# Starting a gated linear attention: the first unit's gates by chunks, with the second unit's steps in their gaps

## The chip, the cores and the metric

The kernel runs on one core of one Trainium2 chip, in float32. The metric is the device time of one execution in microseconds (us). The median of three runs of the kernel before is 581.96 us (580.95 to 583.16).

## The reference, cut to what matters

Two blocks are chained. The first is a gated recurrence over 768 steps for 4 batches of 8 heads of 48 channels, with a complex gate for each channel. The second is a mixture of eight experts, of which each token takes one.

```python
def _attn_ref(q, k, v, a_re, a_im):
    mag = np.sqrt(a_re * a_re + a_im * a_im)
    scale = np.minimum(mag, 0.999) / (mag + 1e-06)
    a_re_n, a_im_n = (a_re * scale, a_im * scale)
    for t in range(S):
        ar, ai = (a_re_n[:, :, t, :, None], a_im_n[:, :, t, :, None])
        new_re = ar * S_re - ai * S_im
        new_im = ar * S_im + ai * S_re
        kv = np.einsum('bhd,bhe->bhde', k[:, :, t], v[:, :, t])
        S_re, S_im = (new_re + kv, new_im)
        y[:, :, t] = np.einsum('bhd,bhde->bhe', q[:, :, t], S_re)

def _moe_ref(x, w_gate, w1, w2):
    logits = x @ w_gate
    expert_idx = np.argmax(logits, axis=1)
    ...                                    # softmax weight of the chosen expert
    for e in range(E):                     # the tokens sorted by expert
        h = np.maximum(x_sorted[lo:hi] @ w1[e], 0.0)
        y_sorted[lo:hi] = h @ w2[e]
    return gate_w[:, None] * y
```

## The kernel before

The recurrence is computed in blocks of 128 steps. A chunk is one block of one batch: 128 steps by 8 heads by 48 channels, which is 384 columns. A unit is two chunks (two batches), W = 768 columns, and there are 12 units. For every unit the kernel needs the running sums of the gate's logarithm and of its angle within the block; both come from a product of TensorE with a triangular matrix. From them follow a decay E with its inverse Ei, and a cosine and sine CS; with these q and k become Q and K, and scores and outputs are matmuls.

The steps of a unit's gates are these. A becomes the logarithm of the capped magnitude, ai the tangent of the angle and later the angle.

```python
    def decay_steps(u):
        ar, ai = T["ar", u], T["ai", u]
        A = un.tile([P, W], FP, tag="A", name="A")
        R = un.tile([P, W], FP, tag="R", name="R", bufs=1)
        T["L", u], T["th", u] = A, ai
        def s0():
            act(out=A, in_=ar, func=AF.Ln)
        def s1():
            act(out=R, in_=A, func=AF.Exp, scale=-1.0)
            nc.vector.tensor_tensor(out=ai, in0=ai, in1=R, op=OP.mult)
            act(out=R, in_=ai, func=AF.Square)
        def s2():
            act(out=R, in_=R, func=AF.Ln, bias=1.0)
            nc.vector.scalar_tensor_tensor(out=A, in0=A, scalar=2.0, in1=R, op0=OP.mult, op1=OP.add)
        def s3():
            act(out=R, in_=A, func=AF.Exp, scale=-0.5, bias=ln2e6)
            nc.vector.scalar_tensor_tensor(out=A, in0=A, scalar=LN_CAP2, in1=R, op0=OP.min, op1=OP.subtract)
        return [s0, s1, s2, s3]

    def decay_angle(u):
        act(out=th, in_=th, func=AF.Arctan)
        ...
    def decay_sums(u, c):                  # chunk c; psM has one buffer
        cs = psM.tile([P, DM], FP, tag="mm", padded_shape=[P, 512], name="csl")
        mm(cs, tri_half, T["L", u][:, sl])
        act(out=T["E", u][:, sl], in_=cs, func=AF.Exp)
        act(out=T["Ei", u][:, sl], in_=cs, func=AF.Exp, scale=-1.0)
        ...
    def angle_sums(u, c):
        cs = psM.tile([P, DM], FP, tag="mm", padded_shape=[P, 512], name="cst")
        mm(cs, tri_turn, T["th", u][:, sl])
        ...                                # r = rounded cs, f = cs - r (DVE)
        if c == U - 1:
            ...                            # fa = |f| over the whole unit (DVE)
    def rotation(u):
        act(out=CS[:, :, 0], in_=fa, func=AF.Sin, scale=2.0 * math.pi, bias=mhalfpi)
        act(out=CS[:, :, 1], in_=f, func=AF.Sin, scale=2.0 * math.pi)
```

ScalarE has one table of functions for logarithm and exponential and another for arctangent and sine. `table(...)` switches it, and the helper `act` keeps the activations of gates in program order. One pass of the loop handles the sums of unit u, the gates of unit u + 1, and the scores of unit u - 1:

```python
    load_a(0)
    load_qkv(0)
    ...                                    # w_gate
    load_a(1)
    table("natural_log_exp_and_others")
    for f in decay_steps(0):
        f()
    table("trig_and_small")
    decay_angle(0)
    for u in range(NU + 1):
        if 0 < u < NU:
            load_qkv(u)
        ...
        if u < NU:
            steps = decay_steps(u + 1) if u + 1 < NU else []
            steps = steps[:1] + [lambda: decay_sums(u, 0)] + steps[1:2] + [lambda: decay_sums(u, 1)] + steps[2:]
            table("natural_log_exp_and_others")
            for i, f in enumerate(steps):
                f()
                ...
            for c in range(U):
                angle_sums(u, c)
            table("trig_and_small")
            rotation(u)
            if u + 1 < NU:
                decay_angle(u + 1)
        ...
        for c in range(U):
            g = (u - 1) * U + c
            if g >= 0:
                scores(g)                  # transposes of Q and K (copies qt, kt), at, am, dk
            if u < NU:
                decayed(u, c)              # Qe = q * E, Ke = k * Ei (DVE)
            if g > 0:
                outputs(g - 1)
        ...
        if u + 2 < NU:
            load_a(u + 2)
```

In `scores` VectorE first multiplies Qe and Ke with CS, which gives Q and K. After the twelve units the tokens' rows, sorted by expert through memory, are loaded again (xg), and the eight experts run as matmuls named hps and yps.

Of the kernel before, what the change touches and what calls it, by code (L numbers as in the profile page):

```python
# [10 lines left out]
FP = mybir.dt.float32  # L11
I32 = mybir.dt.int32
BF = mybir.dt.bfloat16
AF = mybir.ActivationFunctionType
OP = mybir.AluOpType
# [5 lines left out]
P = 128  # L21
MAGIC = 12582912.0
LN_CAP2 = 2.0 * math.log(0.999)
# [14 lines left out]
def kernel(  # L38
# [12 lines left out]
    nc = tc.nc  # L51
    B, H, S, D = q.shape
    DD = 2 * D
    DM = H * D
# [3 lines left out]
    NT = N // P  # L58
    CB = S // P
    U = 2  # L60
    NU = NT // U
    W = U * DM
# [27 lines left out]
    def const(shape, name, dt=FP):  # L90
        return cp.tile(shape, dt, name=name)
# [15 lines left out]
    mhalfpi = const([P, 1], "mhalfpi")  # L107
    nc.vector.memset(mhalfpi, -0.5 * math.pi)

    ln2e6 = const([P, 1], "ln2e6")  # L110
# [47 lines left out]
    T, W_T = {"put": []}, {}  # L158
# [56 lines left out]
    ld = att.enter_context(tc.tile_pool(name="ld", bufs=2))  # L215
    un = att.enter_context(tc.tile_pool(name="un", bufs=2))
# [8 lines left out]
    def act(**kw):  # L225

        ins = nc.scalar.activation(**kw)
        if "act" in T:
            queue(ins, T["act"])
        T["act"] = ins  # L230
# [10 lines left out]
            queue(ins, T["act"])  # L241
        T["act"] = ins

    def load(u, names):
        for nm, src in names:
            if nm == "v":
                t = vbuf[u % 3][:, :, :, 0:D]
                T[nm, u] = vbuf[u % 3]
            else:
                t = ld.tile([P, U, H, D], FP, tag=nm, name=nm, bufs=3 if nm == "ai" else 2)  # L250
                T[nm, u] = t.rearrange("p c h d -> p (c h d)")
            s, b = divmod(u * U, B)
            T["ld"] = nc.sync.dma_start(
                out=t.rearrange("p c h d -> p (c h) d"),
                in_=src[b : b + U, :, s * P : (s + 1) * P, :].rearrange("b h t d -> t (b h) d"),
            )

    def load_a(u):
        load(u, (("ar", a_re), ("ai", a_im)))

    def load_qkv(u):
        load(u, (("q", q), ("k", k), ("v", v)))

    def decay_steps(u):

        ar, ai = T["ar", u], T["ai", u]
        A = un.tile([P, W], FP, tag="A", name="A")
        R = un.tile([P, W], FP, tag="R", name="R", bufs=1)
        T["L", u], T["th", u] = A, ai

        def s0():
# [14 lines that stand above are left out]
            nc.vector.scalar_tensor_tensor(out=A, in0=A, scalar=LN_CAP2, in1=R, op0=OP.min, op1=OP.subtract)  # L286

        return [s0, s1, s2, s3]

    def decay_angle(u):  # L290

        th = T["th", u]
        act(out=th, in_=th, func=AF.Arctan)
        if u * U >= B:
            T["c0", u] = un.tile([96, 8], FP, tag="c0", name="c0")
            nc.gpsimd.dma_start(out=T["c0", u], in_=th[0:1].rearrange("o (p j) -> o p j", j=8))
# [10 lines left out]
    def decay_sums(u, c):  # L307
        sl = slice(c * DM, (c + 1) * DM)
        if c == 0:
            T["E", u] = un.tile([P, W], FP, tag="E", name="E", bufs=1)  # L310
            T["Ei", u] = un.tile([P, W], FP, tag="Ei", name="Ei", bufs=1)
        cs = psM.tile([P, DM], FP, tag="mm", padded_shape=[P, 512], name="csl")
        mm(cs, tri_half, T["L", u][:, sl])
        act(out=T["E", u][:, sl], in_=cs, func=AF.Exp)
        act(out=T["Ei", u][:, sl], in_=cs, func=AF.Exp, scale=-1.0)
        s, b = divmod(u * U, B)
        if s < CB - 1 and c == U - 1:
            if b == 0:
                T["er", s] = un.tile([B, H, 2, D], FP, tag="er", name="er")
            for a in range(2):  # L320
                nc.gpsimd.dma_start(
                    out=T["er", s][b : b + U, :, a],
                    in_=T["E", u][P - 1 : P].rearrange("p (c h d) -> p c h d", c=U, d=D),
                )
# [8 lines left out]
        T["M", s] = un.tile([P, B, H], FP, tag="M", name="M")  # L333
        nc.scalar.copy(out=T["M", s][0:DD], in_=mt[0:DD].rearrange("p h b -> p b h"))

    def angle_sums(u, c):

        if c == 0:
            for nm in ("f", "fa"):
                T[nm, u] = un.tile([P, W], FP, tag=nm, name=nm, bufs=1)  # L340
        sl = slice(c * DM, (c + 1) * DM)
        f = T["f", u][:, sl]
        cs = psM.tile([P, DM], FP, tag="mm", padded_shape=[P, 512], name="cst")
        mm(cs, tri_turn, T["th", u][:, sl])
        r = ch.tile([P, DM], FP, tag="r", name="r")
        nc.vector.tensor_scalar(out=r, in0=cs, scalar1=MAGIC, scalar2=MAGIC, op0=OP.add, op1=OP.subtract)
        nc.vector.tensor_tensor(out=f, in0=cs, in1=r, op=OP.subtract)
        if c == U - 1:
            f, fa = T["f", u], T["fa", u]
            nc.vector.tensor_scalar(  # L350
                out=fa.bitcast(I32), in0=f.bitcast(I32), scalar1=0x7FFFFFFF, scalar2=None, op0=OP.bitwise_and
            )
            if (u + 1) * U <= NT - B:
                T["fl", u] = un.tile([96, 8], FP, tag="fl", name="fl", bufs=3)
                nc.gpsimd.dma_start(out=T["fl", u], in_=f[P - 1 : P].rearrange("o (p j) -> o p j", j=8))

    def rotation(u):

# [6 lines left out]
    def decayed(u, c):  # L365

        sl = slice(c * DM, (c + 1) * DM)
        for nm, src, dec in (("Q", "q", "E"), ("K", "k", "Ei")):
            e = T[nm, u, c] = ch.tile([P, H, D], FP, tag=nm + "e", name=nm + "e")
            o = e.rearrange("p h d -> p (h d)")  # L370
            nc.vector.tensor_tensor(out=o, in0=T[src, u][:, sl], in1=T[dec, u][:, sl], op=OP.mult)
# [170 lines left out]
            nc.sync.dma_start(out=xg[0 : sizes[f], f], in_=rows[:, f * P :].rearrange("o p c -> (o p) c"))  # L542
        return xg

    load_a(0)
    load_qkv(0)
    for z in range(2):
        nc.sync.dma_start(
            out=wg[z * DP : z * DP + D, :, 0:E],
            in_=w_gate.rearrange("(i z d) e -> z d i e", z=2, d=D)[z],  # L550
        )
    load_a(1)
    table("natural_log_exp_and_others")
    for f in decay_steps(0):
        f()
    table("trig_and_small")
    decay_angle(0)
    def place():

        if T["put"]:  # L560
            T["put"].pop(0)()

    for u in range(NU + 1):
        if 0 < u < NU:
            load_qkv(u)
        for i in range(NS // (P * BL)):
            if 2 + i * 2 // (NS // (P * BL)) == u:
                blank(i)
# [7 lines that stand above are left out]
                if i == 1:  # L576
                    carry_angle(u)
            for f in T.pop("chosen", []):
# [7 lines that stand above are left out]
        else:  # L586
            table("natural_log_exp_and_others")
            choose(NT - 2 * GR, GR)()
            T["put"] += route(NT - 2 * GR, False)
            while T["put"]:  # L590
                place()
        if u < NU:
            place()
        for f in T.pop("route", []):
            T["put"] += f()
        for c in range(U):
            g = (u - 1) * U + c
            if g >= 0:
                scores(g)
            if u < NU:  # L600
                decayed(u, c)
            if g > 0:
                outputs(g - 1)
        for _ in range(2 if u >= NU - 2 else 1):
            place()
        if u > 2 and u % 2 and u < NU - 1:

            j = (u - 3) * U
            T["chosen"] = [choose(j, GR)]
            T["route"] = [lambda j=j: route(j, False)]  # L610
        if u + 2 < NU:
            load_a(u + 2)
        if u == NU - 1:
            experts_at(range(2), True)
            load_w(0, range(KD + KF // 2))
# [327 lines left out]
```

## Time and profile before

The engines are PE (TensorE matmul), PEld (its weight loads), DVE (VectorE), ACT (ScalarE), POOL (GpSimd) and SP (SyncE, which issues the loads). Times are us from the start of the profiled execution, whose span is 581.7 us.

| part | what the trace shows |
|---|---|
| until 30 us | gates of units 0 and 1, first loads; no scores yet |
| 30.15 us | first transpose of scores on PE |
| 30 to about 285 us | attention units, one after another |
| 284.55 us | first load of rows for the experts (xg) |
| 288 to 582 us | experts |

A line of the timeline gives the start, the duration, the engine, the line of the program, the operation with its output and input tiles and their shapes, how often it stands there, and in brackets how long the engine was idle before it and what ended the idle time. ACT_TABLE_LOAD is the switch of ScalarE's table; the execution has 27 of them. A row of digits cuts the span into 40 slices of 14.5 us and gives the busy share of each in tenths.

### The profile page before, as it was taken

Reading aid. Unit: us, or ns where it says so; the run is one execution under the profiler, and the core shown is the slowest. Engines: PE = TensorE matmul, PEld = TensorE weight load, DVE = VectorE, ACT = ScalarE, POOL = GpSimd, SP = SyncE. Lnnn points to the kernel's source line nnn. Section 1 sums busy time; section 2 is a strip of 40 time slices with the busy share of each in tenths; the row PEclk is TensorE's granted clock in tenths of the full one; section 3 lists DMA queues with packets and bytes.
Section 4 is the critical chain, followed back from the end, with each engine's and each line's share of the span. In section 5 each row is a group of like instructions: output and inputs, shape, how many; then the busy total and the mean of one; then the engine's idle time right before and its main releaser. Section 6 shows DMA issues by size and latency. Waiting matters only on the chain.

```text
span 581.7 us, 8539 instructions
## 1 busy us (share of the span) xinstructions
PE 538.5 (93%) x3264; PEld 366.0 (63%) x3264; DVE 263.8 (45%) x604; ACT 281.6 (48%) x476; POOL 129.8 (22%) x148
## 2 busy tenths in 40 slices
PE   1499999989999999999799999999999999999995
PEld 0177677678778788687577655555555555555553
DVE  2568877687888879876231211211213022020210
ACT  5677977767777777744210116125162351715210
POOL 2101211231231230201121004215043150604201
PEclk9999999989999999999889999999999999999999
DMA  9999993926854732610443563642736426380001
GB/s 159 182 233 236 257 129 48 177 75 107 150 112 72 135 83 54 231 45 27 152 162 100 177 219 122 210 146 79 271 122 223 153 67 250 122 283 15 25 2 41
DMA packets 151586, 79.31 MB, mean 136 GB/s; under 512 B 127830, under 2 KB 143087, under 8 KB 151536
## 3 DMA queue, kind: packets, MB, share of 16 engines
q1 hardware_dynamic: 146672, 69.04, 50.3%
q0 software_dynamic: 4864, 9.63, 4.9%
q8 instruction: 28, 0.46, 0.4%
q14 instruction: 22, 0.18, 0.1%
HBM read 63.30 MB, written 15.54 MB: 136 GB/s over the span
## 4 chain that ended last, share of the span: by engine, by line
PE 46%; DMA 2%; issue 1%; POOL 1%; ACT 1%; DVE 1%; POOLq 0%; DVEq 0%
PE hps L79 23%; PE yps L79 20%; PE tp L643 2%; DMA xs<-x,slot 2%; POOL cai L732 1%; POOL cs L729 1%; DMA xg<-xs 1%; DVE xt L82 0%; ACT cw L725 0%; ACT cs L725 0%; ACT cai L725 0%; ACT xt L82 0%; DVE y L689 0%; POOL out_dram L654 0%; POOLq L909 0%
## 5 line engine op out<-in xcount | busy, mean ns | idle before, releaser
L79 PE MATMUL hps<-xt,w1t 128*128 128x416 f32 (+4 forms) x432 | 137.5, 478 | 0.0
L79 PE MATMUL yps<-w2t,ht 128*128 128x384 f32 (+2 forms) x464 | 135.1, 487 | 0.0
L79 PEld LDWEIGHTS hps<-xt,w1t 128*128 128x128 f32 x432 | 81.1, 193 | 50.6 <-issue 30.2
L79 PEld LDWEIGHTS yps<-w2t,ht 128*128 128x128 f32 (+2 forms) x464 | 76.3, 178 | 56.7 <-issue 7.4
L674 ACT ACTIVATE ht<-hps 128x416 f32<-128x416 f32 (+4 forms) x36 | 17.1, 475 | 126.9 <-PE hps L79 126.9
L689 DVE TENSOR_SCALAR y<-yps,xg 128x384 f32<-128x384 f32 x24 | 14.8, 617 | 117.3 <-PE yps L79 117.3
L678 DVE TENSOR_SCALAR ht<-hps 128x416 f32<-128x416 f32 (+4 forms) x36 | 19.4, 539 | 90.9 <-PE hps L79 90.7
L79 PE MATMUL at<-qt,kt 96*128 96x128 f32 x384 | 54.9, 285 | 3.5 <-DVE kt L82 2.8
L79 PEld LDWEIGHTS at<-qt,kt 96*128 96x128 f32 x384 | 49.2, 195 | 9.9 <-DVE kt L82 3.3
L79 PE MATMUL y<-am,v 128*64 128x128 f32 x384 | 51.6, 289 | 0.4 <-DVE am L484 0.3
L454 POOL DMA_INDIRECT xs<-x,slot x24 | 26.2, 1094 | 106.7 <-DMA xs<-x,slot 38.3
L654 POOL DMA_INDIRECT out_dram<-y,xg x29 | 28.0, 966 | 92.7 <-DVE y L689 43.7
L79 PE MATMUL y<-qt,G 96*64 96x128 f32 x320 | 46.5, 284 | 0.0
L729 POOL TENSOR_TENSOR cs<-cs,cw 128x768 f32<-128x768 f32 x12 | 21.6, 1804 | 95.8 <-ACT cw L725 95.8
L484 DVE TENSOR_TENSOR am<-at,tri 128x512 f32<-128x512 f32 x48 | 33.0, 686 | 16.9 <-PE at L79 16.6
L79 PE MATMUL csl<-A,tri_half 128*128 128x384 f32 x48 | 24.3, 591 | 17.2 <-DVE A L286 12.8
L79 PEld LDWEIGHTS y<-am,v 128*64 128x64 f32 x384 | 33.8, 138 | 9.5 <-issue 7.8
L79 PEld LDWEIGHTS y<-qt,G 96*64 96x64 f32 x320 | 33.5, 139 | 3.5 <-issue 2.7
L476 PE MATMUL tp<-ident,Q 128*96 128x128 f32 x192 | 33.7, 285 | 2.0 <-DVE Q L376 2.0
L239 ACT ACT_TABLE_LOAD x27 | 34.6, 1283 | 1.2 <-PEq L929 0.8
L82 ACT COPY qt<-tp 96x512 f32<-96x512 f32 x48 | 27.8, 580 | 15.1 <-PE tp L476 14.8
L79 PEld LDWEIGHTS dk<-v,K 128*96 128x96 f32 x320 | 31.0, 170 | 3.8 <-DVE t L514 1.5
(144 smaller groups left out, 747.0 us busy)
## 6 DMA issues: line engine op xcount, KB each, us to landing
w1t<-in_moe_w_dram SPq DMA_DIRECT2D x7, 1536.0 KB, 6.4
w2t<-in_moe_w_dram SPq DMA_DIRECT2D x7, 1536.0 KB, 7.2
xs<-zrow SPq DMA_DIRECT2D x7, 772.0 KB, 8.8
ar<-in_a_re_dram SPq DMA_DIRECT2D x12, 384.0 KB, 5.8
ai<-in_a_im_dram SPq DMA_DIRECT2D x12, 384.0 KB, 6.4
q<-in_q_dram SPq DMA_DIRECT2D x12, 384.0 KB, 6.1
k<-in_k_dram SPq DMA_DIRECT2D x12, 384.0 KB, 6.4
v<-in_v_dram SPq DMA_DIRECT2D x12, 384.0 KB, 4.4
```

Of the source, the lines that this page charges most:

```text
L79: return nc.tensor.matmul(o, lhsT=lhsT, rhs=rhs, start=start, stop=stop, skip_group_check=True)
L82: (nc.scalar.copy if i % 2 else nc.vector.tensor_copy)(out=o, in_=in_)
L239: ins = nc.scalar.preload_act_table_set(name)
L454: pool(nc.gpsimd.indirect_dma_start(out=xs[:, :], out_offset=bass.IndirectOffsetOnAxis(ap=to[:, i : i + 1], axis=0), in_=x[:, i], in_offse ...
L476: nc.tensor.transpose(out=tp[0:DD, j], in_=X[:, hg * 4 + j], identity=ident)
L484: nc.vector.tensor_tensor(out=am, in0=at, in1=bc(tri, 1, 4), op=OP.mult)
L643: t = nc.tensor.transpose(out=tp[:, i * P : i * P + m], in_=xg[0:m, i, d * P : (d + 1) * P], identity=ident[0:m, 0:m],)
L654: T["out"] = nc.gpsimd.indirect_dma_start(out=out, out_offset=bass.IndirectOffsetOnAxis(ap=idx, axis=0), in_=y[0:m], in_offset=None, bound ...
L674: relu = nc.scalar.activation(out=ht[:, f], in_=ps, func=AF.Relu)
L678: nc.vector.tensor_scalar(out=ht[:, f], in0=ps, scalar1=0.0, scalar2=None, op0=OP.max)
L689: nc.vector.tensor_scalar(out=y, in0=ps, scalar1=gate, scalar2=None, op0=OP.mult)
L729: nc.gpsimd.tensor_tensor(out=s, in0=s, in1=w, op=OP.add)
```

## The change

The gates of the first unit are now computed chunk by chunk, each step once for 384 columns and once again, so that a chunk can go on as soon as its own part is there. The steps of the second unit's gates are put between them under the same table, so the extra switches to and from the arctangent's table at the start fall away. The loads are issued in the order of this use: the first unit's ar and ai in halves, then the second unit's ar and ai, then the first unit's q, k and v, then the third unit's ar and ai. R gets a second buffer. The loop then begins at unit 1. The computation stays the same.

The diff, cut to its core (`load` takes a new parameter n, the number of chunks in one transfer; the transfers of er and fl are moved to helpers of their own):

```diff
@@ decay_steps @@
-        R = un.tile([P, W], FP, tag="R", name="R", bufs=1)
+        R = un.tile([P, W], FP, tag="R", name="R")
@@ new @@
+    def first_decay():
+        ...
+        cs = [slice(c * DM, (c + 1) * DM) for c in range(U)]
+        n = decay_steps(1)
+        for c in cs:
+            act(out=A[:, c], in_=ar[:, c], func=AF.Ln)
+            act(out=R[:, c], in_=A[:, c], func=AF.Exp, scale=-1.0)
+            nc.vector.tensor_tensor(out=ai[:, c], in0=ai[:, c], in1=R[:, c], op=OP.mult)
+        for c in cs:
+            act(out=R[:, c], in_=ai[:, c], func=AF.Square)
+            act(out=R[:, c], in_=R[:, c], func=AF.Ln, bias=1.0)
+            stt(out=A[:, c], in0=A[:, c], scalar=2.0, in1=R[:, c], op0=OP.mult, op1=OP.add)
+        n[0]()
+        for c in cs:
+            act(out=R[:, c], in_=A[:, c], func=AF.Exp, scale=-0.5, bias=ln2e6)
+            stt(out=A[:, c], in0=A[:, c], scalar=LN_CAP2, in1=R[:, c], op0=OP.min, op1=OP.subtract)
+        n[1]()
+        decay_sums(0, 0)
+        n[2]()
+        decay_sums(0, 1)
+        n[3]()
+
+    def first_angles():
+        ...
+        for c in range(U):
+            act(out=th[:, c * DM : (c + 1) * DM], in_=th[:, c * DM : (c + 1) * DM], func=AF.Arctan)
+        decay_angle(1)
+        for c in range(U):
+            decayed(0, c)
+        for c in range(U):
+            angle_sums(0, c, True)         # True: fa of this chunk alone
+            ...
+            act(out=CS[:, h, 0], in_=fa, func=AF.Sin, scale=2.0 * math.pi, bias=mhalfpi)
+            act(out=CS[:, h, 1], in_=f, func=AF.Sin, scale=2.0 * math.pi)
+        last_angles(0)
+        last_decays(0)
@@ start @@
-    load_a(0)
+    load(0, (("ar", a_re), ("ai", a_im)), 1)
+    load_a(1)
     load_qkv(0)
+    load_a(2)
     ...                                    # w_gate
-    load_a(1)
     table("natural_log_exp_and_others")
-    for f in decay_steps(0):
-        f()
+    first_decay()
     table("trig_and_small")
-    decay_angle(0)
+    first_angles()
-    for u in range(NU + 1):
-        if 0 < u < NU:
+    for u in range(1, NU + 1):
+        if u < NU:
             load_qkv(u)
```

More of the change, by code (lines that the diff above doesn't have):

```diff
@@ L242, in table, with load @@
         T["act"] = ins
-    def load(u, names):
+    def load(u, names, n=U):
+        ts = []
         for nm, src in names:
@@ L251, in load @@
                 T[nm, u] = t.rearrange("p c h d -> p (c h d)")
[L252 to L256, printed above, removed]
+            ts.append((t, src))
+        s, b = divmod(u * U, B)
+        for c in range(0, U, n):
+            for t, src in ts:
+                T["ld"] = nc.sync.dma_start(
+                    out=t[:, c : c + n].rearrange("p c h d -> p (c h) d"),
+                    in_=src[b + c : b + c + n, :, s * P : (s + 1) * P, :].rearrange("b h t d -> t (b h) d"),
+                )
     def load_a(u):
@@ L288, in decay_steps @@
         return [s0, s1, s2, s3]
+    def first_decay():
+        ar, ai = T["ar", 0], T["ai", 0]
+        A = un.tile([P, W], FP, tag="A", name="A")
+        R = un.tile([P, W], FP, tag="R", name="R")
+        T["L", 0], T["th", 0] = A, ai
+        stt = nc.vector.scalar_tensor_tensor
+        cs = [slice(c * DM, (c + 1) * DM) for c in range(U)]
[18 more added lines that the diff above has]
+    def first_angles():
+        th = T["th", 0]
+        CS = T["CS", 0] = un.tile([P, U * H, 2, D], FP, tag="CS", name="CS")
+        for c in range(U):
[5 more added lines that the diff above has]
+            angle_sums(0, c, True)
+            h = slice(c * H, (c + 1) * H)
+            fa, f = [T[nm, 0].rearrange("p (x d) -> p x d", d=D)[:, h] for nm in ("fa", "f")]
+            act(out=CS[:, h, 0], in_=fa, func=AF.Sin, scale=2.0 * math.pi, bias=mhalfpi)
+            act(out=CS[:, h, 1], in_=f, func=AF.Sin, scale=2.0 * math.pi)
+        last_angles(0)
+        last_decays(0)
     def decay_angle(u):
@@ L315, in decay_sums, with last_decays @@
         act(out=T["Ei", u][:, sl], in_=cs, func=AF.Exp, scale=-1.0)
+        if c == U - 1 and u > 0:
+            last_decays(u)
+    def last_decays(u):
         s, b = divmod(u * U, B)
-        if s < CB - 1 and c == U - 1:
+        if s < CB - 1:
             if b == 0:
@@ L334, in decay_total, with angle_sums @@
         nc.scalar.copy(out=T["M", s][0:DD], in_=mt[0:DD].rearrange("p h b -> p b h"))
-    def angle_sums(u, c):
+    def angle_sums(u, c, each=False):
         if c == 0:
@@ L347, in angle_sums @@
         nc.vector.tensor_tensor(out=f, in0=cs, in1=r, op=OP.subtract)
-        if c == U - 1:
-            f, fa = T["f", u], T["fa", u]
+        if each or c == U - 1:
+            n = sl if each else slice(0, W)
+            f, fa = T["f", u][:, n], T["fa", u][:, n]
             nc.vector.tensor_scalar(
@@ L352, in angle_sums, with last_angles @@
             )
-            if (u + 1) * U <= NT - B:
-                T["fl", u] = un.tile([96, 8], FP, tag="fl", name="fl", bufs=3)
-                nc.gpsimd.dma_start(out=T["fl", u], in_=f[P - 1 : P].rearrange("o (p j) -> o p j", j=8))
+            if not each:
+                last_angles(u)
+    def last_angles(u):
+        if (u + 1) * U <= NT - B:
+            T["fl", u] = un.tile([96, 8], FP, tag="fl", name="fl", bufs=3)
+            nc.gpsimd.dma_start(out=T["fl", u], in_=T["f", u][P - 1 : P].rearrange("o (p j) -> o p j", j=8))
     def rotation(u):
@@ L597 @@
             g = (u - 1) * U + c
-            if g >= 0:
-                scores(g)
+            scores(g)
             if u < NU:
```

## The prediction

> **What bounds the kernel now.** I read the page first: the busy row by engine, then the 40 slices.
>
> ```profile
> PE 538.5 (93%) x3264; PEld 366.0 (63%) x3264; DVE 263.8 (45%) x604; ACT 281.6 (48%) x476; POOL 129.8 (22%) x148
> ...
> PE   1499999989999999999799999999999999999995
> ...
> ACT  5677977767777777744210116125162351715210
> ...
> DMA  9999993926854732610443563642736426380001
> ```
>
> A slice is 14.5 us. TensorE is at nine tenths almost everywhere except in the first two slices, where it stands at 1 and 4. From slice 20 on (from about 288 us) the experts run, and the chain that ended last is TensorE's matmuls there. The change touches nothing of that part. What it can shorten is the start, so I next cut the first 60 us with the windows view. The columns are: stretch, its length, then busy us (instructions) of PE, PEld, DVE, ACT, POOL, then clock, DMA share and GB/s.
>
> ```profile
> 0.00:10.00 10.00, 0.00 (x0) 0.00 (x0) 2.46 (x15) 4.65 (x5) 3.18 (x21) 1.00 1.08 157
> 10.00:20.00 10.00, 3.29 (x4) 1.00 (x4) 3.73 (x5) 7.34 (x9) 0.00 (x0) 1.00 1.40 178
> 20.00:30.00 10.00, 4.94 (x6) 1.50 (x6) 6.59 (x11) 6.53 (x10) 1.95 (x3) 1.00 1.46 179
> 30.00:40.00 10.00, 9.85 (x58) 8.91 (x59) 6.72 (x12) 7.13 (x13) 0.92 (x2) 1.00 1.39 198
> ```
>
> Until 30 us TensorE issues ten matmuls. ScalarE leads: its work on two units' gates, in series with VectorE and loads, decides when the first scores may start. The timeline shows the series:
>
> ```profile
> 4.90 0.84 ACT L227 ACTIVATE A<-ar 128x768 f32<-128x768 f32 x1 [2.87 <-DMA ar<-in_a_re_dram]
> ...
> 11.77 1.28 ACT L239 ACT_TABLE_LOAD   x1
> ...
> 13.93 1.28 ACT L239 ACT_TABLE_LOAD   x1
> ...
> 15.98 0.84 ACT L227 ACTIVATE A<-ar 128x768 f32<-128x768 f32 x1 [0.77 <-DMA ar<-in_a_re_dram]
> 16.73 0.47 ACT L227 ACTIVATE E<-csl 128x384 f32<-128x384 f32 x1
> ...
> 23.65 1.28 ACT L239 ACT_TABLE_LOAD   x1
> ...
> 27.34 0.93 ACT L227 ACTIVATE CS<-fa,mhalfpi 128x768 f32<-128x768 f32 x1 [2.41 <-DVE fa L350]
> ...
> 29.04 0.96 DVE L376 TENSOR_TENSOR Q<-CS,Qe 128x768 f32<-128x768 f32 x1 [1.74 <-ACT CS L227]
> 29.76 1.28 ACT L239 ACT_TABLE_LOAD   x1
> ...
> 30.15 1.06 PE L476 MATMUL tp<-ident,Q 128*96 128x128 f32 x4 [1.73 <-DVE Q L376]
> ```
>
> See four table loads after the one at the start, two of them (11.77 and 13.93) around one lone arctangent; a second unit's logarithm that waits for its load until 15.98; a sine that waits 2.41 us for VectorE; and the first transpose of scores at 30.15. From 4.90 to 29.76 ScalarE idles 7.7 us in six gaps (1.46, 1.03, 0.77, 1.02, 1.03 and 2.41 us). So it is busy about 17.1 of 24.9 us.
>
> **What the Trainium skill says.** "ScalarE: Activation LUTs", section "What ACT_TABLE_LOAD costs": a load of about 1283 ns plus a drain of about 1380 ns. The trace agrees on the load (1.28 us), not on the drain: the arctangent starts at 13.07, 0.02 us after the load that began at 11.77 ended. I therefore count 1.3 us per switch. The same section says that back-to-back activations overlap by about 93 ns; E and its inverse start 0.37 us apart at a duration of 0.47, which agrees. "TensorE: Matmul & The Clock Gate", section on the clock gate: the array runs at half clock until it has been busy for some microseconds. The trace agrees in kind: two csl products of 384 columns take 1.65 us at 12.80, but two cst products take 0.91 at 41.05, although the clock row claims 1.00; I use the slow figure, about 0.83 each, for the start. "DMA: Bandwidth & Descriptors", section "Why small descriptors are slow": short runs pay a fixed cost. The runs here are 48 floats, 192 B, and the first 60 us move 179 to 198 GB/s at a saturated DMA row. So order, not size, decides when an operand lands.
>
> **The change part by part.**
>
> *Step 1, loads.* By windows of 1 us the bytes moved reach 0.44 MB at 4.0 us, 0.82 at 7.0, 1.19 at 8.0 plus a little, then 0.19 MB a us. ar (0.393 MB) lands at about 4.9 and ai (0.786 MB in sum) at 7.05, each some 1.1 us after its last byte. With halves of 0.197 MB the four first chunks land at about 4.05, 4.9, 5.9 and 7.0. The second unit's ar and ai, which now follow at once, land at about 9.05 and 11.1 instead of near 15.9 and 18. q, k and v of the first unit fall back to about 13.2, 15.3 and 17.4; they meet their first reader at about 14.3, so this is off the path. The sum of bytes is the same, so the later loads stay at their times.
>
> *Step 2, the logarithm/exponential table.* A 384-wide activation is 0.47 us, a 768-wide one 0.84; the same VectorE products are 0.55 and 0.96. I walk ScalarE in the order of the compiled program. Ln and Exp of chunk 0 at 4.05 and 4.55; those of chunk 1 wait for data until 5.9 and end at 6.9; two squares and two logarithms of 1+x, alternating, end at 8.9; Ln of unit 1 waits for its load until 9.05 and ends at 9.9; two chunk exponentials to 10.95; Exp of unit 1 to 11.85; its VectorE product to 12.85, an idle 1.05; Square to 13.75; E and its inverse of chunk 0 from 13.78 (their csl product can run from about 11); Ln of unit 1 to 15.4; the second csl product needs the single PSUM buffer and ends at 15.5; E and its inverse to 16.35; the last Exp to 17.3.
>
> *Step 3, the sine table.* Load 17.35 to 18.63. Arctangents of both chunks and of unit 1 from 18.65 to 20.2. cst of chunk 0 to 20.0; VectorE rounds, subtracts and takes the absolute value to 21.5; sines of chunk 0 to 22.4. Chunk 1 goes the same way about 2 us later, and its absolute value stands behind a Q product in VectorE's order, so its sines end at 25.3. First Q about 23.2 (29.04 before, so 5.8 earlier). Next table load at 25.3 (29.76 before, 4.45 earlier).
>
> *Step 4, count check.* Two switches fall away: 2 x 1.28 = 2.6 us of ScalarE. Eight activations of unit 0 become sixteen: 8 x (0.94 - 0.84) = 0.8 us more. The net is 1.8 us less busy. The rest of the 4.45 us is waiting removed: 0.8 of first data half as large, and about 1.9 of idle filled by the other unit's work. The second R buffer is what lets both units' steps interleave.
>
> *Step 5, what reaches the end.* The first score group needs both engines: TensorE could start its transposes 5.4 us earlier, but the copy of qt stands behind the next table load and four activations on ScalarE, so it comes 4.2 to 4.4 us earlier (33.28 before). From there TensorE is busy 95% or more up to 100 us, and its visible waits between 45 and 285 us sum to about 10 us. Nothing in that stretch waits for a time set by the loads: the third unit's ar is issued at 13.27 and is read at 31.05. A shift of the start should travel through. I carry **4.2 us**: 581.96 - 4.2 = 577.8 us, a ratio of 0.993.
>
> **The rivals.**
>
> *A: only the two table loads count.* If unit 1's steps in the gaps delay unit 0's as much as they fill, 1.8 us is left: about 580.2. For it: ScalarE is strictly in order, and a late ar of unit 1 at 9.05 would hold unit 0's exponentials. Against it: my walk has that wait at only 0.2 us.
>
> *B: the loads take over.* The DMA row is saturated for the first 60 us, and compute moves forward while loads do not. q of unit 0 comes 4 us later than before. If it, or a later load, became the wait, the gain would be eaten: 580 to 582. Against it: later operands land 10 us or more ahead of their reader in the trace before.
>
> *C: the attention stage, not its start, sets the pace.* The compiled order differs on every engine through all twelve units (TensorE's list has 712 runs of like instructions against 730), so small waits move. A busy TensorE row contains pipelined latencies and isn't a hard bound. Such shuffles could give back the gain or add to it: some 2 or 3 us either way. The pause at the turn to the experts also leaves the array at half clock (windows 288 to 294 us show 0.50), and where it recovers may differ by a us or two.
>
> *D: the whole 5.4 us of the transposes travels*: 576.5.
>
> **Range and chances.** Centre 577.8. A and B give the upper side (580 to 582), D and a lucky order the lower (574 to 576). The three runs before span 2.2 us. So 574.0 to 581.6 holds it 8 times in 10. Two per cent is 11.6 us: more than twice the gain on one side, and on the other it needs a badly broken order. Faster by over 2%: 0.02; within: 0.97; slower: 0.01.
>
> **What would show it.** In the profile after: 25 table loads instead of 27 (step 4); Ln of unit 1 near 9 us (1, 2); the sine table load near 17.3 (2); first Q near 23 and the next table load near 25.3 (3); the third unit's Ln near 26.6 against 31.05, and the first load of expert rows (xg) some 4 us earlier than 284.55 (5). It would be wrong if the first is met and the last isn't (rival C), or if DMA stands as releaser before Qe or Ke (rival B), or if ScalarE idles for long before Ln of unit 1 (rival A).

## The result, and the profile after

The changed kernel takes 589.95 us (589.5 to 590.68, four runs) against 582.56 us of the kernel before in the same series. The ratio is 1.0125, with an interval of 1.0088 to 1.0162. The forecast was 577.8 us in a range of 574.0 to 581.6: the sign was wrong.

The busy row and the slices come first again, from the page of the changed kernel.

```profile
PE 543.6 (92%) x3264; PEld 367.9 (63%) x3264; DVE 265.1 (45%) x608; ACT 281.1 (48%) x482; POOL 132.5 (23%) x148
...
PE   1597999899999999989899999999999999999995
...
ACT  6696758767887777724310115225152251615210
...
DMA  9999958736853732520262573442735427370001
```

The second slice of TensorE rose from 4 to 5: the start is fuller. But the fourth, from 44.1 to 58.8 us, fell from 9 to 7, and the span is 588.1 us instead of 581.7. The row by itself doesn't tell why.

The timeline of the start answers the lines that were forecast:

```profile
3.69 0.52 ACT L227 ACTIVATE A<-ar 128x384 f32<-128x384 f32 x1 [1.66 <-DMA ar<-in_a_re_dram]
...
9.20 0.84 ACT L227 ACTIVATE A<-ar 128x768 f32<-128x768 f32 x1
...
16.16 0.49 ACT L227 ACTIVATE E<-csl 128x384 f32<-128x384 f32 x1 [1.01 <-PE csl L79]
...
17.87 1.28 ACT L239 ACT_TABLE_LOAD   x1
...
19.73 1.65 PE L79 MATMUL cst<-ai,tri_turn 128*128 128x384 f32 x2 [3.62 <-ACT ai L227]
...
25.40 0.95 DVE L436 TENSOR_TENSOR Q<-CS,Qe 128x768 f32<-128x768 f32 x1
...
26.98 1.06 PE L536 MATMUL tp<-ident,Q 128*96 128x128 f32 x4
...
27.70 1.28 ACT L239 ACT_TABLE_LOAD   x1
```

The first Q is 3.6 us earlier than before, the first transpose of scores 3.2 us, the next table load 2.1 us. And the lead grows. At the fourth unit's first logarithm the changed kernel is at 45.47, the kernel before at 52.48: 7.0 us ahead. Here is what the start of a unit's logarithm (Ln) shows from unit to unit (us, from the timelines):

| unit whose Ln starts | 2 | 3 | 4 | 5 | 6 | 8 | 11 | first xg load |
|---|---|---|---|---|---|---|---|---|
| before | 31.05 | 52.48 | 69.29 | 90.34 | 109.41 | 155.99 | 219.15 | 284.55 |
| after | 28.99 | 45.47 | 69.93 | 94.38 | 113.57 | 155.36 | 218.62 | 291.87 |
| difference | -2.1 | -7.0 | +0.6 | +4.0 | +4.2 | -0.6 | -0.5 | +7.3 |

So the gain is made, and lost between 45 and 70 us; another 3.4 us go before 95. A second loss of nearly 8 us comes after 219. The first is seen in the timeline of the changed kernel:

```profile
44.30 0.54 POOL L346 DMA_DIRECT2D c<-ai  x1 [2.80 <-ACT ls L445]
...
50.78 0.16 DVE L352 SCALAR_TENSOR_TENSOR c<-fl,c 96x8 f32<-96x8 f32 x1 [3.77 <-DMA c<-ai]
50.87 0.68 DVE L82 COPY kt<-tp 96x512 f32<-96x512 f32 x1
51.33 0.51 POOL L355 DMA_DIRECT2D ai<-c  x1 [6.50 <-DVE c L352]
...
51.60 1.09 PE L536 MATMUL tp<-ident,Q 128*96 128x128 f32 x4 [2.90 <-DVE kt L82]
...
52.73 0.58 ACT L82 COPY qt<-tp 96x512 f32<-96x512 f32 x1 [3.97 <-PE tp L536]
```

From unit 2 on, where the second block of 128 steps begins, each unit's angle must go on from the angle where the same batches' last block ended. The helpers `decay_angle` and `carry_angle` do this **carry** with two tiny transfers of 3 KB: c0 (named c in the trace) takes the first row of the new angles out, VectorE adds the last fraction (fl, brought over by a small transfer of its own), and a second transfer puts the row back. Here the first transfer, issued at 44.30, is waited for until 50.78. VectorE takes its instructions in order, so the copy of kt behind it waits too, then TensorE's transposes, then ScalarE's copy of qt. In the kernel before the same transfer took 3.7 us and was waited for 1.09 us:

```profile
51.47 0.54 POOL L296 DMA_DIRECT2D c<-ai  x1 [3.51 <-ACT ai L227]
...
55.16 0.16 DVE L302 SCALAR_TENSOR_TENSOR c<-fl,c 96x8 f32<-96x8 f32 x1 [1.09 <-DMA c<-ai]
```

The difference is the traffic. In the queue's timeline of the changed kernel stand the bulk writes of zeros that prepare the sorted rows; they are issued at the same hour as in the kernel before (37.15), while compute came forward:

```profile
37.18 3.71 SPq L156 DMA_DIRECT2D xs<-zrow  x4
40.99 1.70 SPq L258 DMA_DIRECT2D ar<-in_a_re_dram  x1
42.79 7.80 SPq L258 DMA_DIRECT2D ai<-in_a_im_dram  x1
```

These four writes of 772 KB and two loads began to be issued in the 7 us before the 3 KB are asked for, and such a write has a median of 10.8 us from issue to landing. The windows view (columns as in the prediction) shows what it does to the engines:

```profile
44.00:46.00 2.00, 2.00 (x24) 1.44 (x22) 1.79 (x4) 1.97 (x4) 0.54 (x1) 1.00 1.05 356
46.00:48.00 2.00, 1.94 (x23) 1.80 (x20) 1.02 (x2) 2.00 (x5) 0.00 (x0) 1.00 1.10 321
48.00:50.00 2.00, 0.71 (x2) 0.09 (x1) 0.00 (x0) 0.76 (x2) 0.00 (x0) 1.00 1.16 255
50.00:52.00 2.00, 0.40 (x2) 0.39 (x3) 1.22 (x4) 0.00 (x0) 0.51 (x1) 0.72 0.62 125
52.00:54.00 2.00, 2.00 (x12) 1.98 (x11) 2.00 (x4) 1.27 (x3) 0.00 (x0) 0.50 1.32 215
54.00:56.00 2.00, 2.00 (x11) 1.96 (x11) 1.41 (x4) 1.88 (x5) 1.16 (x2) 0.50 1.45 188
```

Read the third and the last three columns: until 50 us the DMA share is above 1.00, TensorE falls idle, and then the clock stands at 0.50 for some 6 us. A busy TensorE at 2.00 of 2.00 issues 11 or 12 instructions there instead of 24. The pause of 2.9 us is thus paid about once more afterwards.

The second loss has the same shape: the second transfer of the last unit's carry meets the loading of the first expert's weights.

```profile
242.10 3.22 POOL L514 DMA_INDIRECT xs<-x,slot  x1 [0.91 <-DMA xs<-x,slot]
...
245.31 0.55 POOL L355 DMA_DIRECT2D ai<-c  x1
...
252.56 1.62 PE L79 MATMUL cst<-ai,tri_turn 128*128 128x384 f32 x2 [3.62 <-issue]
```

The trace names no releaser but "issue", since the wait ends with the transfer's landing 7.2 us after its issue. In both kernels a scatter (xs<-x,slot) stands ahead of ai<-c in GpSimd's queue. Here it starts 0.4 us after the first weight load (w1t, issued at 241.71) and takes 3.22 us. In the kernel before it starts 0.1 us ahead of that load (237.39) and takes 1.02 us:

```profile
237.30 1.02 POOL L454 DMA_INDIRECT xs<-x,slot  x1 [0.88 <-DMA xs<-x,slot]
...
240.52 0.54 POOL L305 DMA_DIRECT2D ai<-c  x1 [2.20 <-DVE c L302]
...
245.66 0.88 PE L79 MATMUL cst<-ai,tri_turn 128*128 128x384 f32 x2 [0.91 <-issue]
```

### The profile page after: what moved, and what is told of

Its sections match the earlier page's. It is cut to its first block, busy times and chain, and to the rows that moved or that the text cites. A ratio compares the mean times of both kernels' runs of the same rounds, so it can differ in the third digit from the quotient of the medians.

```text
span 588.1 us, 8557 instructions
## 1 busy us (share of the span) xinstructions
PE 543.6 (92%) x3264; PEld 367.9 (63%) x3264; DVE 265.1 (45%) x608; ACT 281.1 (48%) x482; POOL 132.5 (23%) x148
## 4 chain that ended last, share of the span: by engine, by line
PE 68%; DMA 7%; issue 6%; DVE 3%; ACT 2%; POOL 2%; POOLq 0%; DVEq 0%
PE hps L79 23%; PE yps L79 20%; PE y L79 5%; PE at L79 4%; DMA xs<-x,slot 4%; PE tp L536 4%; PE dk L79 3%; PE cst L79 2%; PE tp L703 2%; DMA c<-ai 2%; PE csl L79 1%; DMA q<-in_q_dram 1%; PE tpx L586 1%; POOL cai L792 1%; POOL cs L789 1%
## 5 line engine op out<-in xcount | busy, mean ns | idle before, releaser
L79 PE MATMUL at<-qt,kt 96*128 96x128 f32 x384 | 56.1, 291 | 0.4 <-DVE am L544 0.3
L514 POOL DMA_INDIRECT xs<-x,slot x24 | 28.8, 1202 | 101.9 <-DMA xs<-x,slot 36.3
L79 PE MATMUL y<-am,v 128*64 128x128 f32 x384 | 49.2, 285 | 1.1 <-DVE am L544 1.1
L79 PE MATMUL y<-qt,G 96*64 96x128 f32 x320 | 44.4, 280 | 0.0
L79 PEld LDWEIGHTS y<-am,v 128*64 128x64 f32 x384 | 31.1, 136 | 11.2 <-issue 7.5
L79 PE MATMUL csl<-A,tri_half 128*128 128x384 f32 x48 | 23.6, 575 | 15.0 <-DVE A L315 11.2
L79 PE MATMUL cst<-ai,tri_turn 128*128 128x384 f32 x48 | 24.8, 602 | 10.0 <-issue 4.9
L79 PEld LDWEIGHTS y<-qt,G 96*64 96x64 f32 x320 | 30.6, 137 | 4.0 <-issue 3.1
## 6 DMA issues: line engine op xcount, KB each, us to landing
xs<-zrow SPq DMA_DIRECT2D x7, 772.0 KB, 10.8
```

The lines of the kernel that those rows point to most:

```text
L79: return nc.tensor.matmul(o, lhsT=lhsT, rhs=rhs, start=start, stop=stop, skip_group_check=True)
L514: pool(nc.gpsimd.indirect_dma_start(out=xs[:, :], out_offset=bass.IndirectOffsetOnAxis(ap=to[:, i : i + 1], axis=0), in_=x[:, i], in_offse ...
```

## The experiments

Each run was compared with the kernel before on the same chip. Its medians in the series were 582.56 to 583.89 us. Theory 1 is that the carry's small transfers meet bulk traffic and that what waits for them holds in-order engines. Theory 2 is a worse order of instructions in the whole stage, theory 3 late loads. One edit makes the first four: a condition on the unit.

```diff
-        if u * U >= B:
+        if u * U >= B and u != 2:          # nc2; nc11: u != 11; all: False
```

(in `decay_angle` and in `carry_angle`). These kernels leave out part of the computation: the angles of such a unit start from zero. The carry of unit u is used in the loop's pass u, so what it costs shows at the logarithm of unit u + 2.

**nc2: no carry for unit 2.**

> The changed kernel with the angle's carry left out for unit 2 alone (its angle then starts anew at the third block; the rest is computed as before). Theory 1 (the carry's small transfers are stuck behind the bulk transfers, and what waits for them stands first in an in-order queue): the stretch from 46 to 51 us loses its wait of 3.8 us and the half clock after it, the fourth logarithm of a whole unit (at 69.9 in the changed kernel) comes at 61 to 64, and the whole is 3 to 7 us faster, 583 to 587. Theory 2 (a worse order of instructions in the whole attention stage): within 1.5 us of 590. Theory 3 (the loads themselves are late): the loss between 45 and 70 us stays, 588 to 591.

Measured: 583.24 us, ratio to before 0.9978 (0.9953 to 1.0003). That is 6.7 us below the changed kernel; the twenty runs lie between 578.57 and 590.58. The logarithm of unit 4 comes at 65.88 instead of 69.93, later than expected, because that of unit 3 comes late already (47.69 instead of 45.47). The lead is lost one unit further on: unit 5's comes at 95.01. There the next carry is waited for 3.5 us by VectorE. At unit 11 the profiled execution is level with the changed kernel (218.43 and 218.62). Its gain in the end comes at the last carry, which the edit left in: the scatter ahead of it took 1.01 us here, and cst waited 1.33 us. So the total lies in the expected range by luck.

**nc11: no carry for the last unit.**

> The changed kernel with the carry left out for the last unit alone. Theory 1: the second loss (TensorE waits 3.6 us for the carried angle at 252.6, then half clock) is gone, and the first load of expert rows comes at 284 to 286 instead of 291.9: 582 to 585 us. Theory 2: within 1.5 us of 590. Theory 3: no difference either.

Measured: 587.11 us, ratio 1.0062 (1.0034 to 1.009), 2.8 us below the changed kernel: less than expected. The first xg load did come at 286.82, 5 us earlier, from a unit 11 that was 0.9 us later (219.48): the second loss is gone.

**Without any carry, after and before.**

> The changed kernel without any carry. Theory 1: both losses and the smaller waits for carries are gone: 573 to 579 us, and below the kernel before without carries by the 4 us forecast for the start. Theory 2: the time falls by the same as that of the kernel before without carries, and stays 5 to 9 us above it.

> The kernel before without any carry. Its waits of VectorE for carries sum to 9.7 us, some of them off the path: 576 to 580 us. Theory 1: slower than the changed kernel without carries by 2 to 6 us. Theory 2: faster than it by 5 to 9 us.

Measured: 571.54 us for the changed kernel (0.9802; 0.9774 to 0.9831), below its range, and 577.46 for the kernel before (0.9897; 0.9871 to 0.9923). This is the decisive pair. The changed start is then worth 5.9 us, more than the 4.2 forecast, and it reaches the end. Against it the carries cost 18.4 us in the changed kernel (589.95 - 571.54, from two series whose kernels before differ by 1.2) and some 6 in the kernel before (583.75 - 577.46). Theory 2 asked for the opposite order and falls as the main cause.

**A complete kernel with a cheaper carry.** Only the last row of the fractions is brought over, as one row on partition 0 and two units ahead. VectorE adds it in place.

```diff
-            c0 = T["c0", u]
+            th = T["th", u]
             nc.vector.scalar_tensor_tensor(
-                out=c0, in0=T["fl", u - B // U], scalar=2.0 * math.pi, in1=c0, op0=OP.mult, op1=OP.add
+                out=th[0:1], in0=T["fl", u - B // U], scalar=2.0 * math.pi, in1=th[0:1], op0=OP.mult, op1=OP.add
             )
-            nc.gpsimd.dma_start(out=T["th", u][0:1].rearrange("o (p j) -> o p j", j=8), in_=c0)
```

(fl becomes one row of 768 in two buffers; the transfer that filled c0 goes. For room, R has one buffer again in the changed kernel, and the first unit's R takes the place of fa.)

> The changed kernel, complete, with the carry added in place: the last row of the fractions is brought to partition 0 two units ahead, and one VectorE instruction of 1 x 768 adds it to the first row of the angles; the two small transfers of each carry are gone. (The first unit's R takes the place of its later fa, for room.) Theory 1: the gain of the start reaches the end, less ten VectorE instructions of some 0.8 us more each, of which half lie in gaps: 572 to 578 us. Theory 2 (order): 586 to 592.

> The kernel before with the same carry in place. Theory 1: 577 to 582 us, slower than the changed kernel with it by 3 to 7 us. Theory 2: within 2 us of the kernel before, and faster than the changed kernel with it.

Measured: 577.01 us for the changed kernel (0.9889; 0.983 to 0.9947) and 580.85 for the kernel before (0.994; 0.9914 to 0.9966). The changed start gains 3.8 us where this round trip is gone. The group line and three windows of the changed kernel with this carry show the price and what it buys:

```profile
L349 DVE SCALAR_TENSOR_TENSOR ai<-fl,ai 1x768 f32<-1x768 f32 x10 | 9.4, 940 | 0.4 <-ACT ai L227 0.4
```

```profile
46.00:48.00 2.00, 1.08 (x8) 0.73 (x7) 2.00 (x5) 2.00 (x5) 0.00 (x0) 1.00 1.08 275
48.00:50.00 2.00, 2.00 (x25) 2.00 (x23) 2.00 (x3) 1.46 (x4) 0.00 (x0) 1.00 1.13 277
50.00:52.00 2.00, 2.00 (x18) 1.63 (x17) 1.50 (x3) 2.00 (x5) 0.83 (x2) 1.00 0.80 159
```

VectorE spends 9.4 us on one partition, and is never kept waiting for a carry. TensorE pauses for 0.9 us between 46 and 48, where VectorE is busy throughout, and goes on at full clock through the same traffic.

**blank4: the zeros later.** The edit is `if 4 + i * 2 //` for `if 2 + i * 2 //`. Some zeros then come after the first scatters and erase rows of tokens, and must wait for them, which blurs the total.

> The changed kernel with the seven bulk writes of zeros issued two units later. Theory 1: the carry of unit 2 lands within 4 us instead of 6.5, the fourth logarithm of a whole unit comes at 61 to 65 us instead of 69.9; the writes then meet a later carry, and the second loss stays: 582 to 588 us. Theory 2: 588 to 592.

Measured: 588.59 us (1.0072; 1.0041 to 1.0103), just above the expected range and inside that of theory 2. The step itself holds: ai<-c of unit 2 is issued at 49.0 instead of 51.3, and unit 4's logarithm comes at 65.16 instead of 69.93. Unit 5's comes at 85.31, where the changed kernel without any carry has 85.22: the first loss is gone. The time is lost from unit 6 on; the bulk writes of zeros now begin at 73.86. The last unit's cst still waited, 4.28 us, so the second loss remained.

**The parts alone.** gates_only takes the changed kernel and issues the loads as before; loads_only takes the kernel before and issues them in the new order.

```diff
-    load(0, (("ar", a_re), ("ai", a_im)), 1)
-    load_a(1)
+    load_a(0)
     load_qkv(0)
-    load_a(2)
     ...
+    load_a(1)
```

> The changed kernel with the loads issued as in the kernel before, by whole units. The logarithm of unit 1 waits for its load until about 16 and holds the first unit's last exponentials behind it, so the first Q comes near 29, the next table load near 32: no gain at the start. Theory 1: with the start as late as before, the carries meet the same traffic as before: 580 to 586 us. Theory 2: 587 to 592.

> The kernel before with the new order of loads alone (first ar and ai in halves, then the second unit's, then q, k, v, then the third unit's ar and ai). A logarithm of the whole unit must wait for both halves, about 1 us later than before; the second unit's then no longer waits (0.77 us before). Theory 1: start within 0.7 us of before, so the carries meet the traffic as before: 581 to 586 us. Theory 3 (the new order itself makes loads late): 587 to 592.

Measured: gates_only 592.66 us (1.0154; 1.0091 to 1.0218), a miss upwards, just above the range of theory 2; loads_only 583.63 (1.0005; 0.998 to 1.003), as expected. So the new loads are worth nothing without the gates and hurt nothing. The gates without the loads hold ScalarE, in the timeline of gates_only:

```profile
15.87 0.84 ACT L227 ACTIVATE A<-ar 128x768 f32<-128x768 f32 x1 [6.25 <-DMA ar<-in_a_re_dram]
...
34.41 1.28 ACT L239 ACT_TABLE_LOAD   x1
```

The table load comes 4.7 us later than before, not 2. The first carry lands in 4.2 us, and the stretch from the logarithm of unit 3 to that of unit 5 (52.18 to 91.96) takes 39.8 us. In the changed kernel without any carry it takes 39.7, with all ten 48.9. So with a late start the same order does not have the first loss. The last carry's loss is there all the same: the scatter ahead of it took 3.25 us, and cst waited 3.27 us at 254.3. This loss doesn't hang on how early the start is.

**after_pool: the addition on GpSimd.**

```diff
-            nc.vector.scalar_tensor_tensor(
-                out=c0, in0=T["fl", u - B // U], scalar=2.0 * math.pi, in1=c0, op0=OP.mult, op1=OP.add
-            )
+            nc.gpsimd.tensor_scalar(out=fl, in0=fl, scalar1=2.0 * math.pi, scalar2=None, op0=OP.mult)
+            nc.gpsimd.tensor_tensor(out=c0, in0=fl, in1=c0, op=OP.add)
```

> The changed kernel with the carry's addition on GpSimd instead of VectorE, so that GpSimd waits for the landing and VectorE isn't held. Both small transfers stay. Theory 1: the loss between 45 and 70 us is gone or halved, since GpSimd has nothing urgent; the second loss stays, as the second transfer still stands behind a scatter and the weights: 580 to 586 us. Theory 2: 587 to 592.

Measured: 595.17 us (1.022; 1.0195 to 1.0244). I missed by 9 us and more. Its timeline shows why:

```profile
49.34 1.11 POOL L353 TENSOR_SCALAR fl<-fl 96x8 f32<-96x8 f32 x1 [7.78 <-DMA fl<-f]
50.51 0.58 POOL L346 DMA_DIRECT2D c<-ai  x1
...
57.66 0.98 PE L79 MATMUL cst<-ai,tri_turn 128*128 128x384 f32 x1 [5.55 <-issue]
```

GpSimd is in order too. The scaling of fl, itself a small transfer in the same traffic, now stood ahead of c<-ai, which went out at 50.51 instead of 44.30. The wait moved from VectorE to TensorE's cst: 5.55 us here, and again 3.91 at 164.6 and 3.87 at 255.8. It was no remedy, but it says once more what is waited for.

**after_rank1: the carry as a product.** `mm(cs, ones[0:1], fl_row, False, True)` after the product with tri_turn.

> The changed kernel with the carry as a product of rank one, added in PSUM to the angle's sums: 20 more matmuls of 384 columns from one partition, some 0.4 us each, 8 us of TensorE. Theory 1: no carry is waited for, but TensorE pays: 573 to 581 us. If TensorE isn't the bound of this stage, 572 to 574, as without carries; if it is, 578 to 581. Theory 2: 587 to 592.

Measured: 588.11 us (1.0083; 1.0056 to 1.011), above the range. No carry is waited for, and still the time is nearly the changed kernel's. Its tile view:

```profile
L79 PEld LDWEIGHTS cst<-fl,ones x40: 181/182/184, 54.5 to 251.1; 1*128 1x128 f32 x40
L79 PE MATMUL cst<-fl,ones x40: 481/533/585, 54.5 to 251.4; 1*128 1x384 f32 x40
```

Twenty products are forty pairs of weight load and matmul, 21 us of TensorE by the median and not 8, although one partition carries them. TensorE is busy 254.5 us of the 257 between 28 and 285 us, against 243.6 in the changed kernel: 11 us more. With the carry's waits gone, hardly any idle time of TensorE is left to hide such work in.

**after_mix, before_mix: in place for units 2, 3 and 11 alone.**

> The changed kernel with the carry in place on VectorE for units 2, 3 and 11 alone, whose carries meet bulk transfers, and the small transfers for the other seven. Theory 1: near the version with all carries in place, with less VectorE work but some waits left: 574 to 581 us. Theory 2: 587 to 592.

> The kernel before with the carry in place for units 2, 3 and 11. Theory 1: the start is late, its carries cost little: 578 to 583 us, slower than the changed kernel with the same (576.6) by 2 to 6 us. Theory 2 (order): faster than that one.

Measured: 576.56 us for the changed kernel (0.9888; 0.9862 to 0.9913), level with the version that has all carries in place (577.01); 585.85 for the kernel before (1.0027; 1.0004 to 1.0051), outside its range. The pair again favours the changed start. But the second shows that an in-place carry isn't a gain by itself: the kernel before keeps level until unit 6 and is 2.6 us behind at the first xg load. Its order was reshuffled as well, and which of the two did it wasn't settled.

**Which carries.**

> The changed kernel with the carry left out for unit 2 and the last unit. If the two visible losses are all, this comes to the version without any carry, 571 to 575 us. If the other eight carries cost as well and costs add up (6.7 and 2.8 us were found one by one), 579 to 583 us.

> The changed kernel with the carry kept for unit 2 and the last unit alone. If these two are all of the loss: 586 to 590 us. If costs add up: 18.4 - 9.5, some 9 us below the changed kernel, 579 to 583 us.

Measured: 582.38 us without those of units 2 and 11 (0.9965; 0.994 to 0.9991), 7.6 below the changed kernel; 577.89 without the other eight (0.9915; 0.9884 to 0.9946), 12.1 below and under both of its ranges. The sum, 19.6, agrees roughly with 18.4 for all. That does not mean that each carry has a cost of its own, as the timelines show. The table gives the start of a unit's logarithm less that in the same kernel without any carry (us, one profiled execution each; those of the two kernels of this section took 584.63 and 582.20 us, so read where time is lost rather than how much):

| logarithm of unit | 3 | 4 | 5 | 7 | 11 | first xg load |
|---|---|---|---|---|---|---|
| changed kernel, all ten carries | -0.1 | +6.2 | +9.2 | +11.9 | +13.2 | +18.4 |
| those of units 2 and 11 alone | -0.1 | +6.2 | +6.2 | +6.2 | +6.2 | +11.3 |
| all but those two | -0.2 | -0.2 | +9.1 | +11.2 | +12.5 | +12.1 |
| gates_only, less its later start of 6.7 | 0.0 | +1.2 | +0.1 | +8.5 | +8.7 | +12.3 |
| kernel before, all ten | +0.4 | +0.9 | +0.1 | +4.8 | +7.8 | +4.7 |

The carries of units 2 and 11 alone cost 6.2 and 5.1 us, each at its place. Without them unit 3's carry costs 9.1 us: it now meets the next writes of zeros (three issued from 56.96 on), and VectorE waits for it as it did for unit 2's.

```profile
68.69 0.16 DVE L352 SCALAR_TENSOR_TENSOR c<-fl,c 96x8 f32<-96x8 f32 x1 [3.94 <-DMA c<-ai]
```

In the changed kernel with all ten, where unit 2's carry has already been paid for, the same carry costs 3.0 us more. So the eight are not eight equal costs; about 9 of their 12 us lie at one of them.

## Why the prediction was wrong, by its own steps

*Step 1 (loads) held.* Two of its readings were wrong without harm: 0.82 MB had moved at 6.0 us and not at 7.0, and the first 60 us move from 157 (until 10 us) to 250 GB/s (from 40 to 60), not 179 to 198. The first logarithm was forecast at 4.05 and came at 3.69; that of unit 1 was forecast at 9.05 and came at 9.20. No operand load was waited for after that at the start.

*Step 2 (logarithm table) held*: sine table load at 17.87 against 17.35.

*Step 3 (sine table) had the right chain and one term too small.* I took 0.83 us for a csl or cst product at the start, from a line "1.65 ... x2" that I read as two products. It is one product in two passes: 48 csl instructions serve 24 chunks. The product takes 1.65 us, and it stands in the chain three times: before the second E (ScalarE waits 1.01), before the first r and before the second r. Hence the first Q at 25.40 instead of 23.2 and the table load at 27.70 instead of 25.3. *Rival D* (the whole 5.4 us of the transposes) fell with it: the first transpose came 3.2 us earlier. That the start without carries is worth 5.9 us, more than the 4.2 I had, is in part luck. Of the two kernels without carries the changed one is 2.0 us ahead at the logarithm of unit 2, which is this chain, and 6.5 at that of unit 3, where I had expected nothing more.

*Step 4 (count) held for the loads*: 25 table loads. The page's ScalarE fell by 0.5 us, from 281.6 to 281.1, not by 1.8; one reason is that the chunk activations take 0.51 or 0.52 us in this part and not 0.47.

*Step 5 (what reaches the end) is the step that failed*, in the sentence "A shift of the start should travel through". I looked for waits on operand loads, and there indeed were none: the third unit's ar was early. I did not look at the other transfers. The carry's round trip was in the trace before, as a wait of VectorE of 9.7 us in six places, and as a median of 3.9 us from issue to landing for 3 KB. With compute 7 us ahead of bulk writes that hadn't moved, its landing rose from 3.7 to 6.5 us at unit 2, and that carry cost 6.2 us. In place of a shift that travels through, the runs show a gain of 5.9 us and carries that cost 18.4 us instead of some 6. VectorE's waits for carries do not show this by their sum, which is 9.5 us in four places against 9.7 in six: it matters who stands behind each of them. Rival B named the saturation but looked at the wrong transfers. I also took the few visible waits of TensorE (about 10 us in 240) as proof that a shift would pass. Yet such a wait also costs the low clock that follows. In the traces here the three microseconds after each wait of TensorE of 2.9 us or more, once scores had begun, have a mean granted clock of 0.50 (both losses of the changed kernel) to 0.74 (after a wait of 3.02 us in nc11). Over the whole execution the mean granted clock was 0.981 against 0.990, which is 11.2 us of lost clock in 588.1 against 5.8 in 581.7. If all of that lay on the path, 5.4 of the 6.4 us between the two spans would be clock. That is a bound, worked out from these two means, and no run took the clock away by itself. In the changed kernel with the in-place carry the mean is 0.994.

*Rival A* didn't happen: no idle time stands before unit 1's logarithm. *Rival C* (another order) is not what lost the 9 us until unit 5: with the zeros later (blank4), or with the same order started late (gates_only), 0.1 us is left of them. From unit 5 to unit 11 the carries cost about 4 us in the changed kernel and nearly 8 before, so its loss does not come from there. What stays open is the last carry. From unit 11 to the first xg load it costs 5.2 us in the changed kernel (before, this stretch is 3.1 us shorter with carries than without). The loss is there in blank4 and gates_only too, so neither the zeros nor the early start explain it. The order in GpSimd's queue alone does not either, since the scatter stands at the same place in the kernel before. In the four executions that have this loss with the addition on VectorE, the scatter starts 0.3 to 0.5 us after the first weight load and takes 3.1 to 3.3 us; in before, loads_only and nc2, which don't have it, it starts between 0.1 us ahead of that load and 0.2 us behind it and takes 1.0 us. A meeting by a few tenths of a microsecond fits this, but no run moved it on purpose. Nor did any run issue the carry's transfers from another engine's queue than GpSimd's.

## What to carry to other kernels

When a start is pulled forward, list every transfer that compute waits for later, the smallest first, and ask what will be in the queue at the new hour: the bulk writes here did not move with compute. A round trip by transfers that stands on an in-order engine should be replaced by an instruction in place where that engine has room; here this turned a loss of 1.25% into a gain of 1.1%, though before_mix shows that it needn't be a gain. And count a product by its instructions: "x2" in a group may be two passes of one.

## What the runs showed that I had not expected

A pause of 2.9 us of TensorE (48.7 to 51.6) is followed by some 6 us at half clock, so that the pause costs about twice its length (an estimate; the 6.2 us lost at that place agree). The lead grew from 2.1 to 7.0 us between the logarithms of units 2 and 3. That stretch takes 16.48 us in the changed kernel and 16.48 in gates_only, which starts it at 35.70, against 21.43 in the kernel before and 21.53 in loads_only: it comes with the new gates and not with the earlier hour. In it eight at products at 31.89 took 1.11 us, where the kernel before took 1.88 at 36.47; why was not tested. And a transfer of 3 KB took up to 7.2 us to land beside bulk traffic, with a median of 3.1 us in the same execution.
